# Second expert layer by 512 columns in one bank, the last expert over four column groups, five half-row tiles

## The chip, the cores and the metric

The kernel runs on one core of one Trainium2 chip. The metric is device time in microseconds (us). The kernel before took 180.33 us, the median of three runs (178.92 to 182.07). The engines are named as the profile names them: PE (TensorE, matmuls; PEld its weight loads), DVE (VectorE), ACT (ScalarE), POOL (GpSimd, here the issuer of input DMAs) and SP (SyncE, the issuer of output DMAs).

## The reference

Attention with two kinds of narrow masks feeds a soft mixture of experts. The shapes are q, k, v of (8, 8, 576, 64), phi of (512, 32), w1 of (8, 512, 1024), w2 of (8, 1024, 512), all float32; the output is (4608, 512) float32.

```python
# attention: batch 8, heads 8, sequence 576, head size 64
scores = np.matmul(q, k.transpose(0, 1, 3, 2)) / 8
scores = np.where(masks, scores, -1e9)   # heads 0-3: last 32 positions; heads 4-7: every 4th of the last 128
attn = softmax(scores)
x = np.matmul(attn, v).transpose(0, 2, 1, 3).reshape(4608, 512)

# soft mixture of experts: 8 experts with 4 slots each, 32 slots
logits = x @ phi                          # (4608, 32)
d = softmax over tokens of logits         # dispatch
slot_input = (d.T @ x).reshape(8, 4, 512)
for e in range(8):
    h = np.maximum(slot_input[e] @ w1[e], 0.0)
    slot_out[e] = h @ w2[e]
c = softmax over slots of logits          # combine
return c @ slot_out.reshape(32, 512)
```

## The kernel before, in words

**Order of work.** The program is written as a list of operations (`op`, L118), each with an engine, the buffers it reads and writes, a planned cost and a key. A planner (`Prog.schedule`, L150) places them in time on a model of the engines: of the operations that can start soonest on an engine it takes the one with the lowest key. The order that comes out is the order in which each engine executes, and semaphores are set from it. DMAs of POOL and SP keep the order in which they are written. Where PE would idle in the plan between two given times (`FILL`, L24, in planned us), the planner puts in matmuls whose result nobody uses (`filler`, L1056, the matmul at L1061), as many as fit the gap.

**The main part.** Eight units (two batches by two groups of heads, alternating) pass through: load of q, k, v with a cast to bf16 (POOL DMAs), transposes on PE with evictions on ACT (L570, L565, L591), scores and exponentials (L609, L616), masks on DVE (L624), values and attention output (L634, L639, L663, L672, L674), transposes of the output (L691, L703, L704), logits against phi (`st_L`, L708: matmuls L718, exponential into expT at L723), and the dispatch sums in psA (L749, L762). Between the units' loads POOL issues the experts' weights into WD, stg and TT. They are not waited for until the end. A phi column is 32 wide per column group: `phi_pad` (L532) holds, for each group j of 32 rows, the four slots of expert j in columns 0 to 3 and those of expert j + 4 in columns 4 to 7; the rest is zero. So expT has the 32 slots on partitions 32j to 32j + 7.

**The tail.** Each expert's slots stand in one of four column groups of 32 PE columns: expert e in group e % 4 (experts 0 to 3 in rows 0 to 3 of the group, 4 to 7 in rows 4 to 7). After the last unit:

- psA is copied (L842), folded by matmuls (L849) into siT (L857); the first expert layer (L871) runs 64 matmuls of 512 columns into two banks, relu on ACT and DVE (L878, L881) gives h_sb, four transposes each (L889) and copies (L898) give hT. Between them rsum (L912) makes the combine sums; their reciprocals are rtok (L916).
- The second expert layer is `ffn2` (L925; its matmul is L933). It is done in two column halves `h_` (`CH`, columns 0 to 255 and 256 to 511), each in a PSUM bank of its own (`sp_`). Experts 0 to 5 and a quarter of expert 6 are done for each half; the last six of eight row chunks of expert 6, and expert 7 in two pieces of four chunks, are done for half 0, then, after half 0's output matmuls, for half 1. An expert's matmuls all go to its one column group.
- The last weights are loaded in that order (L832 to L836, issued by the DMA at L468): w25; w26 chunks 0-1 whole and 2-7 of half 0; w27 half 0 in two pieces; w26 chunks 2-7 of half 1; w27 half 1 in two pieces.
- `half` (L971) scales the bank into so_sb (L965, called through `scaled`) and makes `NAB` = 6 half-row tiles of 256 tokens. Tile o has two sub-rows j. Tile 0 has a matmul and an eviction for each j (ACT and DVE) and a store for each. Of the others, the odd ones are evicted by ACT in two steps (L966), the even ones by DVE in one (L1008); each is stored in one piece of 256 KB (1 KB runs of output). All stores are issued by SP in order (L960).
- After both halves, whole rows: groups of 4, 4, 8, 8 times 128 tokens (`GRP`, L902; the loop at L1030), in pairs of 512-column matmuls (L1043), evicted by ACT and DVE in turn (L966, L965) and stored as 1, 1, 2 and 2 MB.

PSUM has eight banks; `psum` (L356) hands them out as tiles of one or two banks, and an operation that needs a bank waits in the plan until one is free.

Of the kernel before, what the change touches and what calls it, by code (L numbers as in the profile page):

```python
# [8 lines left out]
ACTF = mybir.ActivationFunctionType  # L9
F32 = mybir.dt.float32  # L10
# [10 lines left out]
NU = 8  # L21
QB = 96
HALO = 32
FILL = (116.0, 149.0)  # L24


class DmaSem:
# [25 lines left out]
class Op:  # L53
    n = 0
# [248 lines left out]
def bass_dilated_sliding_attn__then__soft_moe_slots_kernel(  # L303
# [12 lines left out]
    op = P.op  # L316

    def sb(name, shape, dt=BF16):
        return A(nc.sbuf_tensor(name, shape, dt))
# [3 lines left out]
    WD = sb("WD", [128, 7, 4096])  # L323
# [16 lines left out]
    phi_st = sb("phi_st", [128, 4, N_SLOTS], F32)  # L340
    phi_pad = sb("phi_pad", [128, 4, 4, 32])
    csum = sb("csum", [128, B], F32)
    rcs = sb("rcs", [128, 1], F32)
# [2 lines left out]
    siT = sb("siT", [128, 2, 4, 4, 32])  # L346
    h_sb = sb("h_sb", [128, FF])
    hT = sb("hT", [128, 2, 8, 4, 32])
    so_sb = sb("so_sb", [128, DM])

    ps = A(nc.psum_tensor("ps", [128, 8, 512], F32))
# [4 lines left out]
    psum = Pool(8, {1: [[6]] + one[:6] + [[7]], 2: [[0, 1], [2, 3], [4, 5], [6, 7]]})  # L356
# [8 lines left out]
    def tile(pool, size=1):  # L365
        t = Buf(pool)
        t.size = size
        return t
# [11 lines left out]
    def bank(t):  # L380
        return ps[:, t.phys[0], :]

    def bankb(t):
        return psb[:, t.phys[0], :]
# [56 lines left out]
    HOME = {}  # L441
# [94 lines left out]
            r=[b_phist], w=[b_phi], cost=0.2, key=1)  # L536
    op("dve", lambda g: g.memset(siT[:], 0.0), w=[b_siT], cost=0.6, key=1)
    op("dve", lambda g: g.memset(hT[:], 0.0), w=b_hT, cost=1.1, key=1)


    U = [dict() for _ in range(NU)]
# [296 lines left out]
    K1 = 1000.0  # L838
# [59 lines left out]
                return en.activation(d_, s_, ACTF.Copy) if p_ == 0 else en.tensor_copy(d_, s_)  # L898
            op("act" if p_ == 0 else "dve", ev, r=[ht], w=[b_hT[p_]], cost=0.3, key=K1)

    NAB = 6
    GRP = [2] * NAB + [4, 4, 8, 8]  # L902
    rs = tile(psum, 1)
    COLS, d_ = [], 0
    for n in GRP:
# [10 lines left out]
    op("dve", lambda vv: vv.reciprocal(rtok[:], bank(rs)[:, 0:N_TOK // 128]), r=[rs], w=[b_rtok],  # L916
       cost=0.2, key=K1 + 1)

    sp_ = [tile(psum, 1), tile(psum, 1)]
    b_sp = [Buf(), Buf()]  # L920
    CH = [slice(0, 256), slice(256, 512)]

    chain = [[], []]

    def ffn2(es_, lo, hi_, h_, key, after=()):  # L925
        pbs = [pb for e in es_ for l2, h2, c0, c1, pb in HOME[f"w2{e}"][1].parts
               if l2 < hi_ and h2 > lo and c0 < CH[h_].stop and c1 > CH[h_].start]

        def pe(t):
            for cc in range(lo, hi_):  # L930
                for e in es_:
                    j, hi = e % 4, e // 4
                    i_ = t.matmul(bank(sp_[h_])[32 * j:32 * j + 32, 0:256],  # L933
                                  hT[:, hi, cc, j, :], w2v[e][:, cc, CH[h_]],
                                  start=(hi == 0 and cc == 0), stop=(hi == 1 and cc == 7),
                                  skip_group_check=True)
            return i_
        o = op("pe", pe, r=[b_hT[0], b_hT[1]] + pbs, alloc=[sp_[h_]] if es_[0] == 0 else [],
               a=[sp_[h_], b_sp[h_]], cost=0.12 * (hi_ - lo), mode="c", key=key, after=chain[h_][-1:] + list(after))
        chain[h_].append(o)  # L940
        for e in es_:
            HOME[f"w2{e}"][1].reads.append(o)

    osts, b_ost = [], []
# [18 lines left out]
    def scaled(en, d_, s_, k_):  # L963
        if en is nc.vector:
            return en.tensor_scalar(d_, s_, k_, None, op0=AluOp.mult)  # L965
        return en.activation(d_, s_, ACTF.Copy, scale=k_)  # L966
# [4 lines left out]
    def half(h_, key):  # L971
        sl = CH[h_]
        mm = []
        e0, e1 = "dve", "act"
        op(e0, lambda en: scaled(en, so_sb[:, sl], bank(sp_[h_])[:, 0:256], rcs[:, 0:1]),
           r=[b_sp[h_], b_rcs, sp_[h_]], w=[b_so[h_]], cost=0.45, key=key)
        for o in range(NAB):
            d0, ap, prev = AB[o]
            k2 = key + 1 + o
# [20 lines left out]
            ob = Buf()  # L1000
            if o % 2:
                for j in range(2):
                    op("act", lambda en, ap=ap, p2=p2, j=j, o=o: scaled(
                        en, ap[:, j, sl], bank(p2)[:, CH[j]], rtok[:, 2 * o + j:2 * o + j + 1]),
                       r=[p2, b_rtok], a=[ob], after=prev, cost=0.4, key=k2)
            else:
                kr = rtok[:, 2 * o:2 * o + 2].unsqueeze(2).to_broadcast([128, 2, 256])
                op("dve", lambda dv, ap=ap, p2=p2, kr=kr: dv.tensor_tensor(  # L1008
                    ap[:, :, sl], bank(p2).rearrange("p (j f) -> p j f", j=2), kr, AluOp.mult),
                   r=[p2, b_rtok], a=[ob], after=prev, cost=0.65, key=k2)  # L1010
            store(d0, 2, ap, ob, k2, h_)
        return mm

    for h_ in range(2):
        k_ = K1 + 2 + 25 * h_
        ffn2((0, 1, 2, 3), 0, 8, h_, k_)
        ffn2((4, 5), 0, 4, h_, k_ + 2)
        ffn2((4, 5), 4, 8, h_, k_ + 2.1)
        ffn2((6,), 0, 2, h_, k_ + 4)
    ffn2((6,), 2, 8, 0, K1 + 10)  # L1020
    ffn2((7,), 0, 4, 0, K1 + 11)
    ffn2((7,), 4, 8, 0, K1 + 12)
    mm0 = half(0, K1 + 20)
    ffn2((6,), 2, 8, 1, K1 + 30, after=mm0)
    ffn2((7,), 0, 4, 1, K1 + 31)
    ffn2((7,), 4, 8, 1, K1 + 32)
    half(1, K1 + 40)

    d0, n0 = 256 * NAB, 2 * NAB
    for i, (n, hs) in enumerate(((4, (3,)), (4, (4,)), (8, (5, 6)), (8, (7, 8)))):  # L1030
        if hs[-1] == 8:
            ap = stg[:, 2, 0:8192].bitcast(F32)
        else:
            ap = WD[:, hs[0]:hs[-1] + 1, :].rearrange("p a x -> p (a x)").bitcast(F32)
        ap = ap.rearrange("p (j f) -> p j f", j=n)
        prev = [x for h in hs for x in b_ost[h]]
        ob = Buf()
# [76 lines left out]
```

## Time and profile before

| what | value |
|---|---|
| runs of the kernel before | 178.92, 180.33, 182.07 us |
| the profiled execution: time, span of its instructions | 178.57 us, 176.8 us |
| mean granted TensorE clock | 0.958 |
| PE, DVE, ACT, POOL busy | 133.8, 113.1, 93.2, 42.3 us |
| HBM read, written | 61.93 MB, 9.44 MB |
| last weight piece lands | 152.95 us |
| first store issued, last eviction ends | 149.84 us, 164.2 us |
| unused matmuls (L1061) | 21 recorded, 121.5 to 142.7 us |

The span runs from the first to the last instruction of the profiled execution; what lies around it is 1.8 us. Busy time of an engine counts stretches with any instruction on it. Idle time of an engine that isn't the one the end waits for costs nothing. In a window's row the last three numbers are the granted clock, the mean busy share of the 16 DMA engines (counted by when packets start, so it can pass 1) and the GB/s they moved. The rate counts what is written to its target: weights are read as float32 and written as bf16.

### The profile page before, as it was taken

Reading aid. Unit: us, or ns where it says so; the run is one execution under the profiler, and the core shown is the slowest. Engines: PE = TensorE matmul, PEld = TensorE weight load, DVE = VectorE, ACT = ScalarE, POOL = GpSimd, SP = SyncE. Lnnn points to the kernel's source line nnn. Section 1 sums busy time; section 2 is a strip of 40 time slices with the busy share of each in tenths; the row PEclk is TensorE's granted clock in tenths of the full one; section 3 lists DMA queues with packets and bytes.
Section 4 is the critical chain, followed back from the end, with each engine's and each line's share of the span. In section 5 each row is a group of like instructions: output and inputs, shape, how many; then the busy total and the mean of one; then the engine's idle time right before and its main releaser. Section 6 shows DMA issues by size and latency. Waiting matters only on the chain.

```text
span 176.8 us, 5764 instructions
## 1 busy us (share of the span) xinstructions
PE 133.8 (76%) x2584; PEld 102.9 (58%) x2590; DVE 113.1 (64%) x260; ACT 93.2 (53%) x142; POOL 42.3 (24%) x80
## 2 busy tenths in 40 slices
PE   0066978885988988997986998888999998597000
PEld 0066767674767867776865977875576566442000
DVE  6820696995678599679489568879943113399100
ACT  2034667743875995765794487577330112499100
POOL 7995302500400520500200020069910000000000
PEclk9999999999999999999999699999999999999755
DMA  4999999999999999999999999999999999999996
GB/s 75 168 235 204 206 216 214 236 213 196 215 213 212 243 208 199 215 221 208 231 221 199 215 213 221 213 215 211 221 204 208 202 196 196 255 344 396 448 430 296
DMA packets 12696, 40.80 MB, mean 231 GB/s; under 512 B 2240, under 2 KB 8896, under 8 KB 9408
## 3 DMA queue, kind: packets, MB, share of 16 engines
q0 software_dynamic: 8272, 30.94, 87.7%
q1 hardware_dynamic: 4400, 9.50, 14.1%
q8 instruction: 20, 0.33, 0.7%
q14 instruction: 4, 0.03, 0.0%
HBM read 61.93 MB, written 9.44 MB: 404 GB/s over the span
## 4 chain that ended last, share of the span: by engine, by line
PE 31%; DVE 23%; DMA 18%; POOL 9%; ACT 8%; issue 3%; POOLq 1%; DVEq 0%
DMA TT<-in_moe_w_dram 14%; DVE PT L624 6%; PE ps L570 6%; DVE XB L674 6%; PE ps L565 5%; PE ps L634 4%; ACT PT L616 4%; DMA stg<-in_v_dram 4%; ACT TT L591 4%; PE ps L718 4%; PE ps L609 3%; DVE WD L965 3%; PE ps L663 3%; DVE VN L639 3%; PE ps L691 3%
## 5 line engine op out<-in xcount | busy, mean ns | idle before, releaser
L591 ACT ACTIVATE TT<-ps 128x864 f32<-128x864 f32 x32 | 28.6, 896 | 30.9 <-PE ps L570 22.0
L616 ACT ACTIVATE PT<-ps 128x768 bf16<-128x768 f32 x48 | 36.9, 814 | 8.7 <-PE ps L609 8.4
L674 DVE TENSOR_TENSOR XB<-ps,RV 96x768 bf16<-96x768 f32 x32 | 30.3, 947 | 0.6
L570 PE MATMUL ps<-ident,stg 96*64 96x96 bf16 x576 | 19.0, 231 | 13.9 <-DMA stg<-in_v_dram 10.5
L570 PEld LDWEIGHTS ps<-ident,stg 96*64 96x64 bf16 x576 | 16.6, 128 | 15.6 <-DMA stg<-in_v_dram 10.7
L639 DVE COPY VN<-ps 128x768 bf16<-128x768 bf16 x32 | 17.4, 545 | 7.6 <-PE ps L634 7.4
L663 PE MATMUL ps<-VN,PT 128*128 128x65 bf16 x384 | 18.1, 196 | 3.2 <-issue 1.1
L703 DVE COPY XT<-ps 128x576 bf16<-128x576 bf16 x19 | 11.4, 598 | 10.9 <-PE ps L691 10.7
L663 PEld LDWEIGHTS ps<-VN,PT 128*128 128x128 bf16 x384 | 14.7, 99 | 5.9 <-DVE PT L624 1.7
L634 PE MATMUL ps<-ident,TT 128*128 128x128 bf16 x192 | 17.1, 231 | 0.6 <-DVE VN L639 0.3
L609 PE MATMUL ps<-TT 64*128 64x96 bf16 x384 | 15.6, 209 | 2.4 <-DVE VN L639 1.0
L691 PE MATMUL ps<-ident,XB 96*128 96x96 bf16 x192 | 13.2, 211 | 3.1 <-DVE XB L674 2.9
L966 ACT ACTIVATE WD<-ps,rtok 128x256 f32<-128x256 f32 (+1 forms) x22 | 9.9, 583 | 9.6 <-PE ps L983 9.6
L565 PE MATMUL ps<-ident,stg 96*128 96x96 bf16 x288 | 14.7, 206 | 0.1
L634 PEld LDWEIGHTS ps<-ident,TT 128*128 128x128 bf16 x192 | 11.7, 103 | 4.5 <-issue 1.3
L609 PEld LDWEIGHTS ps<-TT 64*128 64x128 bf16 x384 | 9.8, 96 | 6.6 <-ACT TT L591 1.2
L624 DVE TENSOR_TENSOR PT<-PT,mask_d 128x768 bf16<-128x768 bf16 x24 | 12.9, 546 | 0.8 <-ACT PT L616 0.4
L691 PEld LDWEIGHTS ps<-ident,XB 96*128 96x128 bf16 x192 | 9.9, 100 | 5.8 <-DVE XB L674 4.9
L565 PEld LDWEIGHTS ps<-ident,stg 96*128 96x128 bf16 x288 | 13.0, 98 | 0.3 <-ACT PT L616 0.3
L624 DVE TENSOR_TENSOR PT<-PT,mask_p 128x768 bf16<-128x768 bf16 x24 | 12.7, 539 | 0.5 <-ACT PT L616 0.5
L704 ACT ACTIVATE XT<-ps 128x576 bf16<-128x576 bf16 x13 | 8.5, 651 | 3.6 <-PE ps L691 3.3
L672 DVE RECIPROCAL RV<-ps 96x12 f32<-96x12 f32 x32 | 7.1, 223 | 4.2 <-PE ps L663 4.2
(90 smaller groups left out, 181.2 us busy)
## 6 DMA issues: line engine op xcount, KB each, us to landing
WD<-in_moe_w_dram POOLq DMA_DIRECT2D x7, 1024.0 KB, 29.6
stg<-in_moe_w_dram POOLq DMA_DIRECT2D x5, 1024.0 KB, 25.0
out_dram<-WD SPq DMA_DIRECT2D x10, 256.0 KB, 2.9
stg<-in_q_dram POOLq DMA_DIRECT2D x4, 576.0 KB, 20.3
stg<-in_k_dram POOLq DMA_DIRECT2D x4, 576.0 KB, 22.8
stg<-in_v_dram POOLq DMA_DIRECT2D x4, 576.0 KB, 25.2
out_dram<-WD SPq DMA_DIRECT2D x2, 1024.0 KB, 5.7
out_dram<-WD SPq DMA_DIRECT2D x1, 2048.0 KB, 9.7
```

The costliest lines, as they stand in the source:

```text
L565: i_ = t.transpose(bankb2(pt, a)[:, 96 * kk:96 * kk + 96], two[:, c, :], ident[0:96, 0:96])
L570: i_ = t.transpose(bankb2(pt, a)[64 * hx:64 * hx + 64, 96 * kk:96 * kk + 96], src[:, hx, c, :], ident[0:96, 0:96])
L591: return ac.activation(d, sv, ACTF.Copy)
L609: i_ = t.matmul(pair(sc)[:, hx, QB * x:QB * x + QB], win(u, 1, h01, blk_, bpar)[64 * hx:64 * hx + 64], win(u, 0, h01, blk_, bpar)[64 * hx: ...
L616: op("act", lambda ac: ac.activation(sbt(pt)[:, 0:768].rearrange("p (x n) -> p x n", x=2), pair(sc)[:, :, 0:384], ACTF.Exp, scale=SCALE), ...
L624: return dv.tensor_tensor(p_, p_, m.unsqueeze(1).to_broadcast([128, 2, 384]), AluOp.mult)
L634: i_ = t.transpose(bankb(pv)[:, 128 * m:128 * m + 128], win(u, 2, h01, m, bpar), ident[:, :])
L639: op("dve", lambda dv: dv.tensor_copy(sbt(vn)[:, :, :, 0:64], bankb(pv)[:, 0:768].rearrange("p (m x d) -> p m x d", m=6, x=2)), r=[pv], w= ...
L663: i_ = t.matmul(pair(po)[:, bk, 65 * po_:65 * po_ + 65], sbt(pts[i])[:, o_:o_ + 128], sbt(vn)[:, m, half, 0:65], start=True, stop=True)
L674: op("dve", lambda dv: dv.tensor_tensor(sbt(xb)[:].rearrange("p m (x h d) -> p h x m d", x=2, h=2)[:, h01], pv()[:, :, :, 0:64], sbt(rv)[: ...
L691: i_ = t.transpose(bankb(px)[:, QB * m:QB * m + QB], sbt(xb)[:, m, 128 * x:128 * x + 128], ident[0:QB, 0:QB])
L703: return en.tensor_copy(d, s_)
```

## The change

- `FILL` shrinks from (116, 149) to (128, 143) planned us.
- `phi_pad` gets a second copy of expert 7's four slots in columns 8 to 11 of every group j. expT has expert 7's slots then on partitions 32j + 8 to 32j + 11 of all four groups as well. A new buffer hT7 (a memset at the start, two copies `ev7` behind those of hT) holds expert 7's hidden activations in columns 8 to 11, for each row chunk.
- `ffn2` takes a list of (expert, chunk). Both halves share one bank. With no half named a matmul has 512 columns. Expert 7's chunk cc goes to column group cc % 4 with hT7, so its sum over chunks is spread over four groups; the output matmuls add the four up, as they sum over all partitions.
- Experts 0 to 5 and chunks 0 and 1 of expert 6 are done for both halves at once, ahead of half 0's last pieces. The rest of expert 6 and expert 7 stay by halves. All calls follow one another in one chain.
- Five half-row tiles instead of six (`NAB`); the whole-row groups are 4, 6, 8, 8 times 128 tokens, laid in WD behind the five tiles. Tile 1's two ACT evictions are stored each by its own DMA.

```diff
@@ -21,7 +21,7 @@
 NU = 8
 QB = 96
 HALO = 32
-FILL = (116.0, 149.0)
+FILL = (128.0, 143.0)
 
 
 class DmaSem:
@@ -346,6 +346,7 @@
     siT = sb("siT", [128, 2, 4, 4, 32])
     h_sb = sb("h_sb", [128, FF])
     hT = sb("hT", [128, 2, 8, 4, 32])
+    hT7 = sb("hT7", [128, 8, 32])
     so_sb = sb("so_sb", [128, DM])
 
     ps = A(nc.psum_tensor("ps", [128, 8, 512], F32))
@@ -536,6 +537,11 @@
             r=[b_phist], w=[b_phi], cost=0.2, key=1)
     op("dve", lambda g: g.memset(siT[:], 0.0), w=[b_siT], cost=0.6, key=1)
     op("dve", lambda g: g.memset(hT[:], 0.0), w=b_hT, cost=1.1, key=1)
+    b_hT7 = [Buf(), Buf()]
+    op("dve", lambda g: g.memset(hT7[:], 0.0), w=b_hT7, cost=0.2, key=1)
+    op("dve", lambda g: g.tensor_copy(
+        phi_pad[:, :, :, 8:12], phi_st[:, :, 28:32].unsqueeze(2).to_broadcast([128, 4, 4, 4])),
+       r=[b_phist], w=[b_phi], cost=0.2, key=1)
 
 
     U = [dict() for _ in range(NU)]
@@ -898,8 +904,14 @@
                 return en.activation(d_, s_, ACTF.Copy) if p_ == 0 else en.tensor_copy(d_, s_)
             op("act" if p_ == 0 else "dve", ev, r=[ht], w=[b_hT[p_]], cost=0.3, key=K1)
 
-    NAB = 6
-    GRP = [2] * NAB + [4, 4, 8, 8]
+        def ev7(en, p_=p_, ht=ht):
+            s_ = bankb(ht)[:, 0:512].rearrange("p (c j i) -> p c j i", c=4, j=4)[:, :, 3, 4:8]
+            d_ = hT7[:, 4 * p_:4 * p_ + 4, 8:12]
+            return en.activation(d_, s_, ACTF.Copy) if p_ == 0 else en.tensor_copy(d_, s_)
+        op("act" if p_ == 0 else "dve", ev7, r=[ht], w=[b_hT7[p_]], cost=0.2, key=K1 + 1)
+
+    NAB = 5
+    GRP = [2] * NAB + [4, 6, 8, 8]
     rs = tile(psum, 1)
     COLS, d_ = [], 0
     for n in GRP:
@@ -916,29 +928,37 @@
     op("dve", lambda vv: vv.reciprocal(rtok[:], bank(rs)[:, 0:N_TOK // 128]), r=[rs], w=[b_rtok],
        cost=0.2, key=K1 + 1)
 
-    sp_ = [tile(psum, 1), tile(psum, 1)]
+    sp_ = tile(psum, 1)
     b_sp = [Buf(), Buf()]
     CH = [slice(0, 256), slice(256, 512)]
-
-    chain = [[], []]
-
-    def ffn2(es_, lo, hi_, h_, key, after=()):
-        pbs = [pb for e in es_ for l2, h2, c0, c1, pb in HOME[f"w2{e}"][1].parts
-               if l2 < hi_ and h2 > lo and c0 < CH[h_].stop and c1 > CH[h_].start]
+    ALL = slice(0, 512)
+
+    chain = []
+
+    def ffn2(items, h_, key, after=()):
+        hs = (0, 1) if h_ is None else (h_,)
+        sl = ALL if h_ is None else CH[h_]
+        pbs = [pb for e, cc in items for l2, h2, c0, c1, pb in HOME[f"w2{e}"][1].parts
+               if l2 <= cc < h2 and c0 < sl.stop and c1 > sl.start]
 
         def pe(t):
-            for cc in range(lo, hi_):
-                for e in es_:
-                    j, hi = e % 4, e // 4
-                    i_ = t.matmul(bank(sp_[h_])[32 * j:32 * j + 32, 0:256],
-                                  hT[:, hi, cc, j, :], w2v[e][:, cc, CH[h_]],
-                                  start=(hi == 0 and cc == 0), stop=(hi == 1 and cc == 7),
-                                  skip_group_check=True)
-            return i_
-        o = op("pe", pe, r=[b_hT[0], b_hT[1]] + pbs, alloc=[sp_[h_]] if es_[0] == 0 else [],
-               a=[sp_[h_], b_sp[h_]], cost=0.12 * (hi_ - lo), mode="c", key=key, after=chain[h_][-1:] + list(after))
-        chain[h_].append(o)
-        for e in es_:
+            for e, cc in items:
+                j, hi = e % 4, e // 4
+                if e == 7:
+                    j, l_ = cc % 4, hT7[:, cc, :]
+                else:
+                    l_ = hT[:, hi, cc, j, :]
+                i_ = t.matmul(bank(sp_)[32 * j:32 * j + 32, sl],
+                              l_, w2v[e][:, cc, sl],
+                              start=(hi == 0 and cc == 0), stop=(e == 7 and cc >= 4),
+                              skip_group_check=True)
+            return i_
+        n = max(sum(1 for e, cc in items if (cc if e == 7 else e) % 4 == g) for g in range(4))
+        o = op("pe", pe, r=list(dict.fromkeys(b_hT + b_hT7 + pbs)), alloc=[] if chain else [sp_],
+               a=[sp_] + [b_sp[x] for x in hs], cost=(0.22 if h_ is None else 0.12) * n, mode="c",
+               key=key, after=chain[-1:] + list(after))
+        chain.append(o)
+        for e in {e for e, _ in items}:
             HOME[f"w2{e}"][1].reads.append(o)
 
     osts, b_ost = [], []
@@ -972,8 +992,8 @@
         sl = CH[h_]
         mm = []
         e0, e1 = "dve", "act"
-        op(e0, lambda en: scaled(en, so_sb[:, sl], bank(sp_[h_])[:, 0:256], rcs[:, 0:1]),
-           r=[b_sp[h_], b_rcs, sp_[h_]], w=[b_so[h_]], cost=0.45, key=key)
+        op(e0, lambda en: scaled(en, so_sb[:, sl], bank(sp_)[:, sl], rcs[:, 0:1]),
+           r=[b_sp[h_], b_rcs, sp_], w=[b_so[h_]], cost=0.45, key=key)
         for o in range(NAB):
             d0, ap, prev = AB[o]
             k2 = key + 1 + o
@@ -1000,9 +1020,15 @@
             ob = Buf()
             if o % 2:
                 for j in range(2):
+                    if o == 1:
+                        ob = Buf()
                     op("act", lambda en, ap=ap, p2=p2, j=j, o=o: scaled(
                         en, ap[:, j, sl], bank(p2)[:, CH[j]], rtok[:, 2 * o + j:2 * o + j + 1]),
                        r=[p2, b_rtok], a=[ob], after=prev, cost=0.4, key=k2)
+                    if o == 1:
+                        store(d0, 2, ap, ob, k2, h_, j)
+                if o == 1:
+                    continue
             else:
                 kr = rtok[:, 2 * o:2 * o + 2].unsqueeze(2).to_broadcast([128, 2, 256])
                 op("dve", lambda dv, ap=ap, p2=p2, kr=kr: dv.tensor_tensor(
@@ -1011,27 +1037,25 @@
             store(d0, 2, ap, ob, k2, h_)
         return mm
 
-    for h_ in range(2):
-        k_ = K1 + 2 + 25 * h_
-        ffn2((0, 1, 2, 3), 0, 8, h_, k_)
-        ffn2((4, 5), 0, 4, h_, k_ + 2)
-        ffn2((4, 5), 4, 8, h_, k_ + 2.1)
-        ffn2((6,), 0, 2, h_, k_ + 4)
-    ffn2((6,), 2, 8, 0, K1 + 10)
-    ffn2((7,), 0, 4, 0, K1 + 11)
-    ffn2((7,), 4, 8, 0, K1 + 12)
+    ffn2([(e, cc) for cc in range(8) for e in range(4)], None, K1 + 2)
+    ffn2([(e, cc) for cc in range(2) for e in (4, 5, 6)], None, K1 + 3)
+    ffn2([(e, cc) for cc in range(2, 8) for e in (4, 5)], None, K1 + 4)
+    ffn2([(6, cc) for cc in range(2, 8)], 0, K1 + 10)
+    ffn2([(7, cc) for cc in range(4)], 0, K1 + 11)
+    ffn2([(7, cc) for cc in range(4, 8)], 0, K1 + 12)
     mm0 = half(0, K1 + 20)
-    ffn2((6,), 2, 8, 1, K1 + 30, after=mm0)
-    ffn2((7,), 0, 4, 1, K1 + 31)
-    ffn2((7,), 4, 8, 1, K1 + 32)
+    ffn2([(6, cc) for cc in range(2, 8)], 1, K1 + 30, after=mm0)
+    ffn2([(7, cc) for cc in range(4)], 1, K1 + 31)
+    ffn2([(7, cc) for cc in range(4, 8)], 1, K1 + 32)
     half(1, K1 + 40)
 
     d0, n0 = 256 * NAB, 2 * NAB
-    for i, (n, hs) in enumerate(((4, (3,)), (4, (4,)), (8, (5, 6)), (8, (7, 8)))):
-        if hs[-1] == 8:
+    for i, (n, hs, o_) in enumerate(((4, (2, 3), 10240), (6, (3, 4), 14336), (8, (5, 6), 20480),
+                                     (8, (7, 8), None))):
+        if o_ is None:
             ap = stg[:, 2, 0:8192].bitcast(F32)
         else:
-            ap = WD[:, hs[0]:hs[-1] + 1, :].rearrange("p a x -> p (a x)").bitcast(F32)
+            ap = WD[:].rearrange("p a x -> p (a x)")[:, o_:o_ + 1024 * n].bitcast(F32)
         ap = ap.rearrange("p (j f) -> p j f", j=n)
         prev = [x for h in hs for x in b_ost[h]]
         ob = Buf()
```

## The prediction

> **What bounds the kernel now.** I read the page's slices first, because they show whether one resource is full from end to end.
>
> ```profile
> span 176.8 us, 5764 instructions
> ...
> DMA  4999999999999999999999999999999999999996
> GB/s 75 168 235 204 206 216 214 236 213 196 215 213 212 243 208 199 215 221 208 231 221 199 215 213 221 213 215 211 221 204 208 202 196 196 255 344 396 448 430 296
> ```
>
> The DMA engines are full from slice 2 to slice 39. Up to slice 34 they bring inputs and weights (some 210 GB/s), after it they take the output away. No compute engine looks like that (PE 76% of the span, DVE 64%). So I looked for the places where the DMA engines are not full: the chain of waits near the end, and the windows around the change from loading to storing.
>
> ```profile
> 128.15 24.80 DMA TT<-in_moe_w_dram
> 152.95 0.04 issue
> 152.99 0.62 PE ps L933 x4
> 153.62 0.02 issue
> 153.64 0.50 DVE so_sb L965
> 154.13 0.05 issue
> 154.18 0.41 PE ps L983 x2
> 154.59 0.02 issue
> 154.61 0.48 DVE WD L965
> ```
>
> The last piece of expert 7's second weight matrix lands at 152.95; four matmuls (L933), the scaling of so_sb and the first output matmuls hang on it, and the first store of the second column half leaves at 155.0. From there the chain follows DVE, but DVE's last eviction ends at 164.2 and the span at 176.8: the last 12 us are stores that drain.
>
> ```profile
> core 0: us, PE busy (x) PEld busy (x) DVE busy (x) ACT busy (x) POOL busy (x), PEclk, DMA share, GB/s
> 153.00:161.00 8.00, 7.26 (x35) 3.37 (x36) 6.87 (x12) 6.50 (x15) 0.00 (x0) 1.00 1.05 345
> 161.00:175.50 14.50, 1.49 (x6) 0.41 (x4) 3.24 (x5) 3.10 (x6) 0.00 (x0) 0.65 1.04 435
> 143.00:150.00 7.00, 6.13 (x122) 4.82 (x122) 1.04 (x3) 0.66 (x2) 0.00 (x0) 1.00 1.45 196
> 150.50:152.50 2.00, 1.27 (x12) 0.89 (x12) 0.67 (x2) 1.50 (x5) 0.00 (x0) 1.00 0.80 180
> ```
>
> Two things are to be seen in the last two columns. Half-row stores (1 KB packets) move at 345 GB/s, whole-row stores (8 or 16 KB) at 435. And between 150.5 and 152.5 the engines are partly idle (share 0.80 against 1.05 and more): the weights run out, and few stores are out yet.
>
> **The change, part by part.** The store traffic sets the end, so each edit is asked when it lets the stores flow and how fast.
>
> *Half tiles, six to five.* 2 x 262,144 B go from half-row to whole-row stores: 0.524 MB / 345 GB/s = 1.52 us against 0.524 / 435 = 1.21. Gain 0.31. All halves together are then 2.62 MB = 7.60 us, 3.80 for each column half, and the whole rows 6.82 MB = 15.67 us.
>
> *Expert 7 over four column groups.* In the timeline its last four matmuls start 0.109 us apart, because they share one column group, and span 0.61. The L871 rows show four groups side by side: seven 512-column matmuls on four groups in 0.61. With four groups the last four of each half end one matmul's 0.28 after the weights land. Gain 0.33 at the head of each half.
>
> *The joint between the halves.* Before, the first store is issued at 149.84 and its first packet moves at 150.69, so 0.85 from issue to packet. The six first-half tiles' packets end at 156.47; the second half's first store, issued at 155.00, could have moved at 155.85: a margin of 0.62. Five tiles end 0.76 us sooner (262,144 B at 345), at 155.71, or at 155.38 if the 0.33 is kept; the second half can move at 155.85 - 0.33 = 155.52. The margin is thus used up, and the joint sits at 155.5 to 155.7. From there 3.80 + 15.67 = 19.47 us to the last packet: 174.99 to 175.18, against 175.40 before. **Gain 0.2 to 0.4 us; I take 0.4**, since the shorter matmul group that brings the second half forward brings the first one forward too.
>
> *The second tile in two pieces.* Two 128 KB stores where there was a 256 KB one. 128 KB stores land 0.40 to 0.43 us apart in the trace, 256 KB ones 0.75, so a split costs below 0.1 in a full queue. It lets the third store leave before ACT has done both halves (150.71 before, some 0.4 sooner now), into the gap of 150.5 to 152.5. That gap holds 0.6 us of full-rate work. I give it no gain: what leaves sooner only makes the joint wait for the second half. Bounds: 0.1 lost, 0.6 gained if the second half comes sooner too.
>
> *Experts 0 to 5 by 512 columns.* All their second-layer work now stands ahead of the first half's last pieces. By L871, four 512-column matmuls take 0.216 together: 8 x 0.216 + 2 x 0.216 + 6 x 0.216 = 3.46, then six of expert 6 at 0.109 = 0.65 and four of expert 7 in 0.12: 4.23 us. The start was 143.00, behind the unused matmuls (L1061). The two new copies into hT7 go behind those that end at 142.26 (ACT) and 142.45 (DVE); at 0.24 each they end at 142.7, and the planner fills that wait with at most one more unused matmul, 0.2: start 143.2. So PE is ready at 147.4; the first half's last weight piece lands at 147.78. Cost nothing, covered by 0.35 us of waiting. Past that each us is late for the first half.
>
> *Evictions.* DVE and ACT get 13 whole-row evictions each for 12 (0.67 us on DVE, where eight take 5.35): the last store is issued 0.3 later. Nothing: that store queues behind a 2 MB one which drains until 170.5. The memset of hT7 and the copy into phi_pad sit in the first 14 us, where DVE waits for the inputs.
>
> *Fewer unused matmuls.* The planner's window loses some 12 of them, at 121 to 128.
>
> ```profile
> core 0: us, PE busy (x) PEld busy (x) DVE busy (x) ACT busy (x) POOL busy (x), PEclk, DMA share, GB/s
> 93.70:97.10 3.40, 1.81 (x59) 1.52 (x57) 3.37 (x8) 1.16 (x2) 0.00 (x0) 1.00 0.90 190
> 97.10:100.50 3.40, 3.40 (x68) 3.19 (x68) 1.60 (x3) 1.55 (x2) 0.00 (x0) 0.50 1.03 217
> ...
> 121.00:124.40 3.40, 2.85 (x46) 1.64 (x47) 3.37 (x8) 1.62 (x2) 3.40 (x8) 1.00 1.01 212
> 124.40:127.80 3.40, 3.21 (x38) 1.94 (x37) 3.37 (x7) 1.04 (x2) 3.40 (x5) 1.00 1.07 222
> ...
> 151.70:155.10 3.40, 1.60 (x14) 1.14 (x14) 0.97 (x3) 0.89 (x3) 0.00 (x0) 1.00 0.85 272
> ```
>
> The clock halves from 97.1 to 100.5 after a stretch in which PE was busy for 1.81 of 3.40 us, and stays whole after 151.7 to 155.1 with 1.60. Without the unused matmuls (L1061 covers 1.53 and 1.22 of the two stretches) 121.0 to 124.4 has some 1.7, 124.4 to 127.8 some 2.2, so a half clock from 124.4 to 127.8 is about an even chance. It costs at most half of that stretch, 1.7 us of PE, less what DVE (3.37 of 3.40 busy) hides. The first half's stores then start up to 1.3 later, yet the weights, with no stores beside them, are through sooner: 152.95 less 0.49 (their last piece took 1.83 where others of its size take 1.34). From 152.4 on, 7.60 + 15.67 = 23.3 us of stores end at 175.7. I take nothing, with 0.3 as the upper bound. [...]
>
> Sum: the last packet moves 0.4 us sooner, span 176.4. The profiled execution took 178.57, its span 176.8 and 1.8 around it; it lies 1.8 below the median of the runs, 180.33. Taken from the median: **179.9**.
>
> **The rivals.**
>
> *The last weight piece lands later (slower).* Place: the weights' queue at 150 to 153. Stores of the first half that leave sooner share the engines with the last pieces. The 0.24 MB of stores moved before 152.5 stretched the last piece by 0.49. Two further 128 KB stores ahead of it cost another 0.54; all that is left of the half, 1.07 MB, would cost 2.2. Above 0.4 the gain is gone, since the joint waits for the second half. Taken at 0.9: 180.8. For it: the pieces go out earlier. Against: the gap shows many engines idle. [...]
>
> *It lands sooner.* An instruction fetch (queue q8, one 16 KB packet) falls at 150.6 among the last pieces. The page has 20 such packets for 5,174 PE and PEld instructions, one for 259. The change drops about 64 matmuls with their loads, 128 instructions, and 98 of them were left after 150.6, so that fetch may go. With the last piece at 152.2 and the gap filled, the joint is at 154.8: 0.9 to 1.1 sooner, 179.3. Against: nothing shows that the fetch delayed the slowest engine.
>
> *PE is late beyond the cover.* Two stretches of half clock or a worse order in the planner: PE 3.4 us late, less the cover of 0.35; the first store at 149.51 + 3.05 = 152.6, packets from 153.4, the last at 176.7, that is 1.3 later: 181.6. It decides from some 2 us of lateness, where packets start at 152.1. Against: 97.1 to 100.5 shows PE busy throughout at half clock and whole again after it.
>
> *The four groups don't run side by side.* Then the joint is 0.33 later and the gain 0.1: 180.2. Against: L871.
>
> **Numbers.** Forecast 0.47 (179.9), later piece 0.24 (180.8), sooner piece 0.14 (179.3), late PE 0.09 (181.6), no overlap 0.06 (180.2). The cases lie between 179.3 and 181.6 and the runs of one kernel between 178.92 and 182.07, 1.4 below and 1.7 above their median. I give 177.9 to 182.2. About 2% is what a measurement of this kernel can tell from no change, and no case moves it by 3.6 us: within 2% 0.87; faster by more 0.05, slower by more 0.08, both from the spread, the latter with late PE.
>
> **What would show it.** Right: the last L933 group of each half spans 0.3; the L1061 rows between 121 and 128 are gone; the last load lands within 0.3 of 152.95; the second half's first store leaves near 154.7; span 176.0 to 176.8. Wrong: PE reaching expert 7's first half after 148; a last load past 153.4; a half clock beyond one stretch; a DMA share well under 1 between 155 and 157; stores that wait for DVE after 160.

## The result

The changed kernel takes 180.11 us (median of 21 runs, 179.22 to 185.73), the kernel before 178.92 (21 runs, 178.16 to 182.07). The ratio is 1.0062, 95% interval 1.004 to 1.0084: **slower by 0.6%**, some 1.1 us, where 0.4 less was forecast. Measured a second time, the changed kernel gave 1.0086 (1.0049 to 1.0122). Runs more than 1.5% above the fastest of their kernel are left out of the ratios, so lowest and median of all runs are given beside them.

The profile first taken of the changed kernel is of an execution of 183.25 us. The lines below come from its second run, of 181.44 us, to be set against 178.57 for the profiled execution before. Both stand above the median of 180.11, so this profile shows 2.9 us of loss where the runs show 1.1. New line numbers are L951 for the second layer, L985 and L986 for evictions, L1003 and L1016 for the output matmuls, L1085 for unused matmuls. First the page's slices:

```profile
span 179.6 us, 5639 instructions
...
PEclk9999999999999999999999999998559999999555
DMA  4999999999999998999999999999999998899994
GB/s 65 186 224 223 201 215 211 238 201 207 218 213 214 238 217 187 221 215 214 233 213 197 221 212 221 212 213 219 212 205 221 187 199 111 277 334 421 424 467 182
```

Three places differ from before: the clock is half in slices 29 and 30, slice 34 moves 111 GB/s where 196 were moved, and the last slice has 182 for 296. The windows give them in time:

```profile
core 0: us, PE busy (x) PEld busy (x) DVE busy (x) ACT busy (x) POOL busy (x), PEclk, DMA share, GB/s
121.40:124.80 3.40, 1.86 (x48) 1.38 (x44) 3.37 (x9) 1.82 (x3) 3.40 (x7) 1.00 1.00 210
124.80:128.20 3.40, 2.74 (x33) 2.38 (x30) 3.22 (x7) 0.65 (x1) 3.40 (x6) 0.50 1.05 219
128.20:131.60 3.40, 3.16 (x30) 2.28 (x29) 1.79 (x5) 1.39 (x3) 1.52 (x3) 0.50 1.05 203
131.60:135.00 3.40, 3.07 (x21) 1.42 (x21) 1.05 (x5) 0.74 (x2) 0.00 (x0) 0.50 1.05 212
135.00:138.40 3.40, 3.35 (x50) 2.00 (x49) 1.25 (x2) 0.00 (x0) 0.00 (x0) 0.99 1.02 214
150.50:152.50 2.00, 1.40 (x14) 1.08 (x13) 1.44 (x3) 1.06 (x3) 0.00 (x0) 1.00 0.24 32
153.00:161.00 8.00, 7.20 (x35) 3.23 (x33) 7.38 (x13) 7.11 (x16) 0.00 (x0) 1.00 0.92 303
161.00:175.50 14.50, 1.74 (x6) 0.45 (x5) 3.66 (x6) 2.73 (x5) 0.00 (x0) 0.66 1.01 424
177.60:178.80 1.20, 0.00 (x0) 0.00 (x0) 0.00 (x0) 0.00 (x0) 0.00 (x0) 0.50 0.03 14
```

The clock is half for 10.2 us, not for one stretch of 3.4. The DMA engines stand at a share of 0.24 from 150.5 to 152.5 (0.80 before): the last weight packets end at 151.6 and the first store's packets start at 152.8. And over the last 1.2 us the share is 0.03, less than the one sixteenth (0.06) that one engine makes up: fifteen of the sixteen DMA engines are done, and **one moves its last packets alone**. (In the first profile the last three 16 KB packets follow one another and end at 179.42, 180.03 and 180.64, with no other 16 KB packet beside the last two.) In the last 1.2 us before, the engines ended together, with a share of 0.52:

```profile
174.80:176.00 1.20, 0.00 (x0) 0.00 (x0) 0.00 (x0) 0.00 (x0) 0.00 (x0) 0.50 0.52 219
```

The chain of waits shows the first part of the loss:

```profile
145.71 1.03 PE ps L1085 x4
146.73 3.81 PE ps L951 x52
150.55 0.03 issue
150.57 0.49 DVE so_sb L985
151.07 0.05 issue
151.12 0.39 PE ps L1003 x2
...
152.38 1.00 PE ps L951 x12
```

PE begins the second layer at 146.73 (143.00 before) and is through at 150.55, while expert 7's last first-half weights have been there since 147.23. No DMA stands in this part of the chain, where before the last weight piece did. The first store leaves at 151.94, 2.10 later than before.

The second part is in the DMA queues from 160.5 to 162 us, in the middle of the stores:

```profile
DMA packets 357, 0.58 MB, mean 386 GB/s; under 512 B 31, under 2 KB 324, under 8 KB 324
...
q8 instruction: 1, 0.02, 4.4%
```

This is the instruction fetch that stood at 150.63 before, under the weight loads. It starts at 160.82 and holds one DMA engine for 1.06 us, and the half-row store that lands next comes 2.23 us behind the one ahead of it, where the two before it came 0.78 and 0.80 behind theirs. The time from first store to last packet is 26.84 us, against 26.19 before.

### The profile page after: what moved, and what is told of

It reads as the page before. It is cut to its first block, busy times and chain, and to the rows that moved or that the text cites. A ratio compares the mean times of both kernels' runs of the same rounds, so it can differ in the third digit from the quotient of the medians.

```text
span 181.4 us, 5639 instructions
## 1 busy us (share of the span) xinstructions
PE 134.3 (74%) x2522; PEld 102.4 (56%) x2526; DVE 114.1 (63%) x264; ACT 92.4 (51%) x140; POOL 42.3 (23%) x80
## 4 chain that ended last, share of the span: by engine, by line
PE 46%; DVE 27%; ACT 7%; issue 4%; DMA 4%; POOL 3%; DVEq 0%; POOLq 0%
DVE XB L680 7%; DVE PT L630 7%; PE ps L576 6%; PE ps L724 6%; PE ps L640 5%; PE ps L571 5%; DVE VN L645 4%; PE ps L697 4%; PE ps L615 4%; ACT PT L622 4%; DVE WD L985 4%; DMA stg<-in_v_dram 4%; POOL stg L434 3%; PE ps L669 3%; PE ps L951 3%
## 5 line engine op out<-in xcount | busy, mean ns | idle before, releaser
L697 PE MATMUL ps<-ident,XB 96*128 96x96 bf16 x192 | 13.8, 217 | 3.5 <-DVE XB L680 3.5
L697 PEld LDWEIGHTS ps<-ident,XB 96*128 96x128 bf16 x192 | 10.6, 104 | 5.9 <-DVE XB L680 4.6
L986 ACT ACTIVATE WD<-ps,rtok 128x256 f32<-128x256 f32 (+1 forms) x19 | 9.1, 604 | 6.4 <-PE ps L1003 6.4
L724 PE MATMUL ps<-XT,phi_pad 128*128 128x192 bf16 (+1 forms) x64 | 12.0, 345 | 0.1
```

The source lines that it names most:

```text
L697: i_ = t.transpose(bankb(px)[:, QB * m:QB * m + QB], sbt(xb)[:, m, 128 * x:128 * x + 128], ident[0:QB, 0:QB])
L724: i_ = t.matmul(o_, phi_pad[:, c].rearrange("p j i -> p (j i)"), rhs, start=c == 0, stop=c == 3)
```

## The experiments

The theories, with their letters in the expectations. **Clock** (A): fewer unused matmuls leave the clock at half, PE is late, the stores begin late. **Columns** (B): the 512-column matmuls of experts 0 to 5 use up the cover ahead of expert 7. **Joint** (C): five half tiles leave the store queue empty between the halves. **Both** (D, formed later): clock and columns cost only together. **Fetch** (formed when these left a rest): the twentieth instruction fetch has moved from the loads into the stores, and one DMA engine ends late. Each profile of a kernel below has its own run's clock, so single profiles are compared only for what follows a given event. "Lowest" and "median" are of all runs.

**Parts done and undone.** The first edit, alone:

```diff
-FILL = (128.0, 143.0)
+FILL = (116.0, 149.0)
```

> The changed kernel with the unused matmuls planned from 116 to 149 as before, nothing else undone. Theory A (the missing unused matmuls let the TensorE clock fall near 121 to 137, PE is late and the first store with it): the clock is whole from 121 to 144, PE reaches expert 7's first half before 148.5, the first store leaves by 150, and the time falls below the kernel before, ratio 0.996 to 1.000. Rival B (the 512-column matmuls ahead of the first half's last pieces make PE late by themselves): the first store still leaves after 150.5 and the ratio stays at 1.003 to 1.008. Rival C (the stores are the cause: five half tiles leave the store queue empty at the joint of the halves): a DMA share under 0.6 remains between 155 and 157, ratio 1.003 to 1.006.

Ratio 0.9998 (0.9962 to 1.0034), median 179.02, lowest 178.40. With the old window of unused matmuls and all else changed, the loss is gone: the 512 columns, the five tiles and the rest don't carry it by themselves. But the early start that the clock theory asked for didn't come: in the profile (180.57 us) the clock is whole from 51 us on, and still the second layer begins at 146.52 and the first store leaves at 151.79, where it was to leave by 150. The reverse, the kernel before with `FILL = (128.0, 143.0)`:

> The kernel before with only the planner's window for unused matmuls cut to 128 to 143. Theory A: a half clock of 3.4 us or more between 121 and 137, the first store 0.5 to 4 us later, ratio 1.004 to 1.012. Rivals B and C: no change in time, ratio 0.998 to 1.002, whatever the clock does.

0.9992 (0.9948 to 1.0035), lowest 177.95, but a median of 180.02 where the kernel before, measured beside it, had 179.07, and 5 of 12 runs at 181.07 or more. So the window by itself makes runs uneven without lifting the floor, and doesn't explain why no run of the changed kernel is under 179.2.

Columns undone, by 256 columns in two banks, with the old window and with the new one:

```diff
-    sp_ = tile(psum, 1)
+    sp_ = [tile(psum, 1), tile(psum, 1)]
...
-    ffn2([(e, cc) for cc in range(8) for e in range(4)], None, K1 + 2)
+    for h_ in range(2):
+        k_ = K1 + 2 + 25 * h_
+        ffn2([(e, cc) for cc in range(8) for e in range(4)], h_, k_)
...
```

> The changed kernel with the old window for unused matmuls and with the second expert layer by halves of 256 columns in two banks in the old order; expert 7 over four groups, five half tiles and the split second tile stay. Theory A: the same time as with 512 columns and the old window, within 0.2%. Rival B: this one is 0.4 to 0.8% below it. Rival C: the same time as it, both above before.

> The changed kernel with the second expert layer by halves of 256 columns in two banks in the old order; the short window for unused matmuls, expert 7 over four groups, five half tiles and the split tile stay. So far the short window alone costs nothing in the interval (0.9992, though its runs spread from 177.95 to 184.65) and the rest of the change without it costs nothing (0.9998). Theory D (both together: the half clock makes PE late, and the 512-column matmuls put 0.5 to 1 us more work between a late start and the first half's last matmul, so that no run escapes): the lowest time falls from 179.2 to below 178.6 and the ratio to 0.998 to 1.002. Theory A alone (the clock, whatever the order of the second layer): ratio 1.004 to 1.010, lowest time 179 or more.

1.0005 (0.9973 to 1.0038) with the old window, level with the 512 columns. With the new one 0.999 (0.9957 to 1.0024), lowest 178.24, median 180.08: much like the new window in the kernel before. That the floor is back at 178.24 looked like a point for the columns; but this kernel issues 50 more matmuls, each with its load, and its fetch is back at 154.12, before the first store of that run (154.61). Laid side by side, these are the four cases of window and columns:

| unused matmuls | columns | ratio | fetch at |
|---|---|---|---|
| old window | 256 | 1.0005 | 150.53 |
| old window | 512 | 0.9998 | 154.16 |
| new window | 256 | 0.999 | 154.12 |
| new window | 512 (the changed kernel) | 1.0062, 1.0086 | 161.83, 160.82 |

Neither part costs by itself, and both together do. That fits theory D, and it fits the fetch as well: each part takes PE instructions away (the columns 50 matmuls with their loads, the window 15), and only with both gone does the fetch come after 160. The run with forty tiny matmuls below tells the two apart.

Expert 7 over four groups, alone, in the kernel before:

```diff
+                if e == 7:
+                    j, l_ = cc % 4, hT7[:, cc, :]
+                else:
+                    l_ = hT[:, hi, cc, j, :]
```

> The kernel before with expert 7 over four column groups alone (phi_pad's second copy, hT7 and its two copies, expert 7's chunks by cc % 4); halves, six half tiles and the old window stay. The forecast's step: the last four matmuls of each half span 0.28 to 0.35 us where they spanned 0.61, the first store of each half leaves 0.3 sooner, ratio 0.998 to 1.000. If the two copies into hT7 delay the start of the second layer by more than that, the ratio is 1.000 to 1.003.

1.0006 (0.9973 to 1.0039): no change within the interval, which can't tell a gain of 0.3 us (0.2%) from none.

**How many unused matmuls.** The changed kernel with none (`FILL = (900.0, 901.0)`), and with all that fit between planned 20 and 149 us:

> The changed kernel without any unused matmul. Theories A and D: more half clock between 120 and 145 and a first store after 152.5, median above 181, ratio 1.008 to 1.02. If the unused matmuls do not matter, and it is the order of the real ones: 1.004 to 1.008, as the changed kernel.

> The changed kernel with the window for unused matmuls from 20 to 149: 26 more of them before 116 than with the old window. If a half clock earlier in the pipeline (near 44 and 97) is what leaves PE late in the runs above 179, the highest time falls from 182 to below 180.5, the median to 178.2 to 178.8, ratio 0.995 to 0.999. If those matmuls get in the way of real ones instead: ratio 1.000 to 1.004.

None: 1.0168 (1.0128 to 1.0208), lowest 180.60. All: 0.9976 (0.9949 to 1.0003), lowest 178.34. Its clock is whole from 23.2 to 166.6:

```profile
span 177.2 us, 5725 instructions
...
PEclk9999999999999999999999999999999999999755
DMA  4999999998999999999999999999999999899996
```

The wide window with 256 columns, and that with the planner's smallest gap to be filled at 0.28 in place of 0.4 us:

> The same wide window with the second layer by halves of 256 columns in two banks. Theory D: with the clock kept up the columns make no difference, within 0.2% of the wide window with 512 columns. If the 512-column matmuls cost by themselves, this one is 0.3 to 0.6% lower.

> The wide window (20 to 149) with halves of 256 columns, and gaps from 0.28 us filled where it was 0.4, which adds one unused matmul at 127. If single gaps near 127 still let the clock fall: median 178.4 to 178.7, ratio 0.995 to 0.998. If not: as the wide window with halves, 0.997 to 0.999.

0.9975 (0.9951 to 0.9998) and 1.002 (0.9985 to 1.0056). The first against 0.9976 says again that 512 or 256 columns make no difference; the second lies above both ranges that were given for it, so that filling smaller gaps too brought nothing. Then the two ends of the old window by themselves, 116 to 143 and 128 to 149, beside the changed kernel once more:

> The changed kernel with the window for unused matmuls from 116 to 143: of the 15 unused matmuls that the change drops, the 12 planned before 128 are back, the 3 planned at 146.4 (between expert 7's first half and the output matmuls) stay out. Theory A (what was lost is the clock of 121 to 137): ratio 0.997 to 1.002, lowest time below 178.7, as with the whole old window. If it is the 3 late ones: ratio 1.004 or more, lowest time 179 or more.

> The counterpart: the window from 128 to 149, the 3 late ones back, the 12 early ones out. Theory A: as the changed kernel, median 179.8 to 180.5, ratio 1.004 to 1.009, lowest time 179 or more. If it is the 3 late ones: ratio 0.997 to 1.002.

> The changed kernel as it is, beside the two others on one chip, for its profile: theory A expects a half clock of one stretch of 3.4 us or more between 121 and 137 in every execution, and a first store 0.7 us or more after the 149.84 of the kernel before; median 179.8 to 180.5.

1.0121 (1.0074 to 1.0167), 1.0112 (1.0074 to 1.0149), 1.0086. This is where the clock theory alone broke: it had 0.997 to 1.002 for the first of these. The profile with 128 to 149 begins its second layer at 143.65 and its first store leaves at 149.08, sooner than before, yet it needs 27.97 us from there to the last packet. Its fetch stands at 166.01, and at the end one engine works alone again, for 1.7 us:

```profile
175.20:177.06 1.86, 0.00 (x0) 0.00 (x0) 0.00 (x0) 0.00 (x0) 0.00 (x0) 0.50 0.06 26
```

Laid side by side, every profile with a fetch at 160 or later has this lone engine, and none of the other sixteen profiles has it:

| kernel | fetch at | first store | from there to last packet | one engine alone at the end | lowest |
|---|---|---|---|---|---|
| before | 150.63 | 149.84 | 26.19 | under 0.2 | 178.16 |
| all changed, old window | 154.16 | 151.79 | 26.22 | under 0.2 | 178.40 |
| window 116 to 143 | 154.66 | 151.79 | 26.68 | under 0.2 | 180.34 |
| changed, second run | 160.82 | 151.94 | 26.84 | 1.2 | 179.64 |
| changed, first run | 161.83 | 153.65 | 26.99 | 1.2 | 179.22 |
| window 128 to 149 | 166.01 | 149.08 | 27.97 | 1.7 | 179.68 |
| no unused matmuls | 166.99 | 152.56 | 27.26 | 1.2, and two engines for 0.4 before it | 180.60 |

The fetch moves with the number of PE instructions ahead of it: in these rows it comes after 5,016 to 5,076 recorded matmuls and weight loads, at whatever time that is.

**One row stays outside this.** The window 116 to 143 is 1.2% slower than the kernel before (six runs, none under 180.34), and its profile (181.01 us) has neither a half clock between 121 and 137 nor a fetch after 160. Its fetch took 1.53 us, where that of the old window took 0.88; with the same first store the last packet came 0.46 us later. That is a fifth of its 2.2 us. The rest of this loss stays open: the clock of its profile was half from 44.3 to 47.7, and whether it was in the other five runs is not on record.

**The fetch by itself.** Forty tiny matmuls at the start of PE, before any data has come, in the changed kernel:

```diff
+    t_pad = tile(psum, 1)
+
+    def pad(t):
+        for _ in range(40):
+            i_ = t.matmul(bank(t_pad)[0:32, 0:1], ident[:, 0:32], ident[:, 0:1], start=True, stop=True)
+        return i_
+    op("pe", pad, r=[b_id], w=[t_pad], alloc=[t_pad], cost=1.20, key=-5)
```

> The changed kernel with 40 tiny unused matmuls (32 columns of weights, 1 column through) on PE at the start, before the first data arrive at 13.6 us; all else is the changed kernel's. They move the twentieth instruction fetch some 80 instructions forward, from 161.8 us among the stores to before the last weight has landed. Theory fetch among the stores: no store then lands more than 2 us behind the one before it, the lowest time falls from 179.2 to 178.0-178.7, and the ratio of the undisturbed runs to 0.998-1.003; the clock's lower stretch before 137 us stays, and with it a median of 179.2-180.5. Rival, the 512 columns or the clock alone set the floor: the lowest stays at 179.2 or above and the ratio at 1.005-1.012.

0.9996 (0.9965 to 1.0027), median 179.22 as the kernel before measured beside it, lowest 178.40. Clock and fetch of its profile:

```profile
123.70:127.10 3.40, 2.92 (x40) 2.58 (x37) 3.25 (x6) 0.65 (x1) 3.40 (x5) 0.50 1.04 217
127.10:130.50 3.40, 3.17 (x30) 2.24 (x28) 1.96 (x5) 1.39 (x3) 1.79 (x3) 0.50 1.05 215
130.50:133.90 3.40, 3.07 (x24) 1.63 (x24) 0.95 (x4) 0.74 (x2) 0.00 (x0) 0.50 1.05 200
175.60:176.80 1.20, 0.00 (x0) 0.00 (x0) 0.00 (x0) 0.00 (x0) 0.00 (x0) 0.50 0.52 218
```

The DMA queues from 150.5 to 151.7 have the fetch:

```profile
q8 instruction: 1, 0.02, 4.7%
```

The clock is half for the same 10.2 us, but the fetch is at 150.74, all engines end together (0.52), and first store to last packet is 25.87. All other recorded instructions stand on each engine in the order of the changed kernel. Forty matmuls whose result nobody uses take the whole measured loss away, with the half clock and the 512 columns still there: that speaks for the fetch against theory D. A fetch is one packet of 0.02 MB, and there are 20 in the page before for 5,174 recorded matmuls and weight loads, one for 259. It costs nothing that shows at the end in the profiles with the fetch under the loads (a share of 0.52 over the last 1.2 us, here and before), and goes with one engine alone for 1.2 to 1.7 us in the four with a fetch at 160 or later.

As a control 20 of them in the kernel before; and 100, and then 82, which add a twenty-first fetch there:

> The kernel before with 20 tiny unused matmuls at the start: the twentieth fetch comes a little before 150.6 us, under the weight loads still, and no further one follows. Both theories: ratio 0.997-1.003, lowest 178.0-178.5. A ratio above 1.004 would say that the unused instructions at the start cost by themselves, and would take the worth from the other two runs.

> The kernel before with 100 tiny unused matmuls at the start: a twenty-first fetch comes some 50 instructions before its last, among the stores, at 156-162 us. Theory fetch among the stores: one store lands 1 to 2 us late, the lowest is 178.8 or above, the ratio 1.004-1.012, with the clock at the end no lower than before. Rival, the fetch is hidden: lowest 178.0-178.5, ratio 0.998-1.003.

> The kernel before with 82 tiny unused matmuls at the start, 18 fewer than in the earlier run, so that the twenty-first fetch comes some 12 instructions before PE's last, at 159 to 162 us, in the full store queue. Theory fetch in the full queue: one store lands 1 us or more late, one DMA engine alone moves the last packets, 1.0 to 1.6 us after the others have ended, the lowest is 178.8 or above and the ratio 1.004-1.010. Rival, such a fetch is hidden at any place among the stores: lowest 177.7-178.4, ratio 0.997-1.002.

The control: 0.9985 (0.9956 to 1.0014); the tiny matmuls cost nothing themselves. **The other two missed their aim.** Both profiles have the added fetch at 154.77, not at 156 to 162, and the ratios are 0.9989 (0.9953 to 1.0025) and 1.0001 (0.997 to 1.0031), lowest 177.74 and 178.11. So a fetch among the first stores needn't cost anything, and the half of the theory that says it costs in any kernel's full queue was not tried on the kernel before. Nor is it settled why 154.7 cost nothing there and went with 1.0121 in the window 116 to 143, whose fetch is at 154.66. A late store alone says little: one lands 1.90 us behind the one ahead with 100 tiny matmuls and 2.93 with 82, and there all engines end together. The count of instructions missed the place by 1.2 and 4.2 us, taken from the near ends of the two ranges.

**A better version, and what the rest of the change is worth.** The wide window with 24 tiny matmuls in the changed kernel, and the wide window in the kernel before:

> The changed kernel with unused matmuls in every gap between 20 and 149 us (as in the earlier wide run) and 24 tiny ones at the start, which move the fetch from 151.2 to about 148 us. Theory fetch among the stores: in the wide run it came with the last weight and cost at most 0.3 us; ratio 0.994-0.999. Rival, it was hidden there: 0.996-1.000, as that run's 0.998.

> The kernel before with its window for unused matmuls opened to 20-149 us, as in the wide runs of the changed kernel; its fetch stays under the weight loads. If the changed tail (halves, tiles, column groups) is worth its 0.4 us, this comes out behind the changed kernel's wide run with 24 tiny matmuls (0.9951): 0.996-1.000. If the tail is worth nothing: 0.993-0.997, level with it.

0.9951 (0.9928 to 0.9975), median 178.32, lowest 177.86: **faster than both kernels**, by 0.5% against the one before. The kernel before gains nothing by the wide window: 1.0019 (0.9994 to 1.0045), above both ranges that were given for it. Against the forty tiny matmuls measured beside it (0.9996) the wide window is worth 0.45%, 0.8 us, to the changed kernel (the two intervals overlap by 0.001).

## Why the prediction was wrong

**Fewer unused matmuls** is the first step that failed; it was costed at nothing, at most 0.3. Its reading of the row was right (121.4 to 124.8 has PE busy for 1.86 of 3.40, then the clock is half), its length was not: it took one stretch, because 97.1 to 100.5 came back whole, but there PE was busy for 3.40 of 3.40. Here PE was busy for 2.74, 3.16 and 3.07 in three stretches at half clock, and only after the third was the clock whole again. PE was ready at 150.55 for 147.4. What these 10.2 us cost in time is not shown. The wide window is worth 0.8 us, but it fills gaps from 20 us on, where other profiles have half clocks too; and the old window, with a whole clock from 121 to 137, is level with the forty tiny matmuls, with a half clock there (0.9998 and 0.9996).

**"That fetch may go"** is the step that decided. The sum had no term for the fetch; it stood in the rival of a sooner piece alone. The count was right (98 instructions left, 126 recorded ones dropped for 128), the conclusion was not: the fetch came all the same, with 12 recorded instructions left, in another run with 16, in two further kernels with none left. It did not go, it went from the loads to the stores. The rival priced only its absence, at 0.9 to 1.1 sooner; no case had it later. With the fetch back under the loads, and the order of all other instructions as it was, 1.0062 and 1.0086 became 0.9996: within that interval it accounts for the whole loss.

**PE is late beyond the cover** (0.09) came in both profiled executions: its first store at 152.6 lies between the measured 151.94 and 153.65, and its 181.6 near their 181.44 and 183.25, but above the median of 180.11. But it has the stores flow at full rate from the first packet, 23.3 us to the last. The run with the fetch out of the way has 25.0 (151.81 to 176.82; 24.4 to the start of the last packet, from which the 175.40 of the sum was read): with the weights gone, 151 to 155 has shares of 0.37, 0.62, 0.78 and 0.72, since the stores come no faster than their tiles (SP waits for the evictions of ACT and DVE there). Lateness is forgiven less than that sum says: the first store 1.79 later than in the best version (150.96 for 149.17), the last packet still 1.32 later (176.82 for 175.50).

**Last load within 0.3 of 152.95, and later as a rival.** It landed at 151.94, 1.0 sooner: with no stores beside it the piece wasn't stretched (1.38 us for 1.83). The rival of a later piece did not come, nor the share well under 1 between 155 and 157 (0.97 and 1.05); the hole was at 151 to 153.

**Experts 0 to 5 by 512 columns cost nothing**: right. With the clock whole the best version runs them from 143.16 (143.2 forecast) to 146.9, and PE then waits 0.56 for expert 7's weights. What they did cost came by the way that the step left out: 50 matmuls and loads fewer, and so a later fetch.

**Expert 7 over four groups** gained what was said at this place in the chain. The chain of the best version and of the kernel before with the same window:

```profile
152.09 0.04 issue
152.13 0.32 PE ps L959 x4
```

```profile
152.32 0.04 issue
152.37 0.62 PE ps L933 x4
```

0.32 for 0.62. The first store also leaves 1.75 us after the first half's last weights have landed, for 2.06.

**The joint, 0.4**: right in kind, too large. From those weights' landing to the last store's is 28.61 us before, 28.75 with the wide window, and 28.42 and 28.44 in the two wide runs of the changed kernel: 0.2 to 0.3 gained. What is missing lies at the joint, which the sum had full. The windows of the best version, then of the kernel before with the wide window:

```profile
154.00:156.00 2.00, 2.00 (x10) 1.08 (x8) 1.47 (x3) 1.68 (x4) 0.00 (x0) 0.50 0.87 294
156.00:157.00 1.00, 1.00 (x5) 0.52 (x4) 0.84 (x3) 0.78 (x2) 0.00 (x0) 0.77 0.58 192
```

```profile
154.00:156.00 2.00, 2.00 (x15) 1.28 (x13) 2.00 (x4) 2.00 (x6) 0.00 (x0) 1.00 1.04 344
156.00:157.00 1.00, 0.90 (x4) 0.15 (x3) 1.00 (x3) 1.00 (x4) 0.00 (x0) 1.00 1.05 341
```

Five tiles end sooner than the second half's stores can follow: 0.58 for 1.05 from 156 to 157. (In this run the clock was half for one stretch from 153.05; the other wide run, with a whole clock, has 0.77 from 157 to 158.) The rates were right: 345 GB/s in half-row stores, 425 to 432 in whole rows. **The second tile in two pieces** and the **evictions** were costed at nothing; no run tried either alone.

So the change is in itself a small gain, 0.2 to 0.3 us in the profiles. (The ratios of the wide runs, 0.9951 and 0.9976 against 1.0019, would make it 0.4 to 0.7%, but they were measured on different chips, and their intervals are as wide as that.) The smaller window that came with it let the clock fall, and window and columns together, by the lower count of instructions, moved a fetch to where it costs.

## What to carry to other kernels

Before instructions are taken away, count where the instruction fetches fall and where they will fall (the count was off by up to 4 us here): with the end set by a full store queue here, a fetch of one 16 KB packet between 160.82 and 166.99 went with one of sixteen DMA engines alone at the end for 1.2 to 1.7 us, and forty tiny matmuls at the start, which moved it to 150.74, took the ratio from 1.0062 and 1.0086 to 0.9996. Look at the DMA share of the last microsecond: 0.03 to 0.06 there was one engine alone in these profiles, whatever the mean said. And unused matmuls that keep the clock whole are priced by how long it stays half without them, 10.2 us here, not by one stretch.

## What the hardware showed beside this

With a fetch of 1.06 us in the middle of a full queue, one DMA engine ended 1.2 us behind the other fifteen, some 18 us later. With the fetch at 166.01 it was 1.7 us, more than the packet's own 0.93. That this engine is the one that moved the fetch is the author's reading; no run shows it. The clock also fell to half near 44 us in some profiles, for 3.4 or 6.8 us: in the changed kernel's first run and not in its second, and in the run with the old window, whose second layer began at 146.52 with the clock whole from 51 us on. All seven profiles with a half clock that begins between 43.8 and 44.7 us are of executions of 180.29 us or more, with the first store at 151.79 or later, that of the window 116 to 143 among them; the one that begins at 42.1 is of 178.21. How much of the spread between runs of one kernel this is was not measured.
